# A residual block with two normalised convolutions: the first image's normalisation, its loads and its PE warm-up reordered tile by tile

## Chip, cores and metric

The kernel runs on one core of one Trainium2 chip. The time is device microseconds (us) per execution. Before the change it was 293.24 us (median of 6 executions, 292.82 to 293.89). Single outliers exist (one execution of the kernel before took 418 us); they count as slow and are left out.

Names used below: PE is the tensor engine (matmuls, and transposes done as matmuls), PEld its weight loads, DVE the vector engine, ACT the scalar engine, POOL the GpSimd engine, SP the engine that issues most DMA loads. The span is the length of the one execution that the profiler recorded. "Cold" and "warm" name two speeds of PE that the traces below show, the cold one about half the warm one.

## The reference

```
# x: 2 x 512 x 32 x 32, G = 4 groups of 128 channels, all bf16
def gn(z, gamma, beta):            # per image and group of 128 channels
    mu, var = mean and variance of z over the group
    return (z - mu) / sqrt(var + 1e-5) * gamma + beta
h = conv3(silu(gn(x, g1, be1)), w1)        # 3x3, 512 -> 512 channels
h = h + (silu(t_emb) @ w_emb)              # one number per image and channel
h = conv3(silu(gn(h, g2, be2)), w2)
out = x + h
```

One group has exactly 128 channels, so it is one SBUF tile of 128 partitions. An image has four such tiles. The statistics of one tile do not depend on another tile.

## The kernel before

The parts that matter are the order of each engine's work before the first convolution. Weights arrive as output rows by input columns and are transposed on PE, 36 blocks of 128x128 per chunk, in five sets (8, 8, 8, 8, 4) called `("T", chunk, set)`. After each set ACT or DVE copies it out of PSUM. "tot1" is the small matmul that sums a tile's statistics over partitions. "v1" and "sb1" are the two halves of the scale chain on DVE, with a power step ("rs1") on POOL between them. "sig" is the sigmoid on ACT and "mul" the multiply on DVE that writes the padded input of the convolution.

```
# PE list (cut)
pe_list.append(("tot1", 0))                 # all four tiles of image 0 in one matmul
pe_list.append(("gbT",))                    # transpose of gamma/beta
for s_ in range(3): pe_list.append(("T",) + c0 + (s_,))
# ... six warm-up matmuls, then the first convolution group, with inserts:
#     after input tile 0: T sets 3, 4;  after input tile 2: ("tot1", 1) for image 1

# PE, "tot1": waits for every tile of the image
eng.wait_sem(sem_dve, max(EV("dve", ("st1", b * CT + ct)) for ct in range(CT)))

# PE, convolution: input tile by input tile, in order
for cit in range(CT):
    wait_input(cit)                         # weight copies of this tile, and its "mul"
    for tap in range(9):
        for ph in range(NPH):               # two halves of 512 pixels
            e.matmul(acc_bank(s_, ph), lhsT, pad_window(src_buf, jt, dy, dx, ph), ...)
    for k2 in inserts.get(cit, []):
        emit(k2)

# SP (cut)
dma_x(0); dma_w(0, 0); dma_w(0, 1); dma_x(1)   # image 0, weight chunks, image 1
# POOL (cut): constants, then the four loads of g1, be1, g2, be2, then the zero borders
```

## Time and profile before

| what | value | where to read it |
|---|---|---|
| time | 293.24 us; span of the profiled execution 291.0 | times; first line of the page |
| PE busy | 278.4 us, 96% of the span | part 1 of the page |
| first convolution matmul | 15.42 us | chain of waits |
| end of the first convolution group | 32.36 us | chain of waits |
| 18 matmuls of 512 columns, array warm | 3.98 us, 0.221 each | chain of waits |

The first lines of the page of the kernel before. The "busy tenths" line cuts the span into 40 slices of 7.3 us, and each digit is the busy share in tenths.

```profile
span 291.0 us, 3566 instructions
PE 278.4 (96%) x1575; PEld 139.6 (48%) x1575; DVE 71.8 (25%) x189; ACT 59.5 (20%) x75; POOL 14.3 (5%) x29
PE   0699999999999999999999999999999999999996
```

PE is saturated from the third slice on. Only the first two slices, and the very end, have room.

This is the chain that ended last in the kernel before, up to the second group: the work followed back from the last instruction, each piece waiting for the one before it. Columns: start, duration, engine and tile written, source line, count.

```profile
1.64 4.03 DMA x_sb<-in_x_dram
...
5.69 1.30 DVE bn L738 x2
...
9.47 0.57 PE stat_ps L915 x2
...
10.15 1.87 PE tp L905 x16
...
13.23 1.25 ACT s_buf L655
...
14.58 0.71 DVE xn_pad L784
...
15.42 4.13 PE acc L983 x18
19.56 0.73 PE tp L905 x12
20.29 7.96 PE acc L983 x36
28.25 0.12 PE stat_ps L915 x2
28.37 3.99 PE acc L983 x18
32.36 0.94 PE stat_ps L940 x36
```

Read it downwards. The path goes through the load of x, DVE's statistics of two tiles, one statistics matmul for all tiles, 16 transposes, the sigmoid and the multiply. From 15.42 us on every piece is PE. Compare the two transpose lines: 16 take 1.87 us (0.117 each) at 10 us, and 12 take 0.73 us (0.061 each) at 19.6 us. The array is cold in the first and warm in the second.

### The profile page before, as it was taken

What the parts mean: (1) busy time and instruction counts of PE and PEld (TensorE: products, weight loads), DVE (VectorE), ACT (ScalarE), POOL (GpSimd) and SP (SyncE); (2) the same over time, 40 slices, a digit from 0 to 9 for tenths busy, and PEclk for the clock granted to TensorE, in tenths of its full rate; (3) what the DMA queues carried; (4) which work ended last, traced back from release to release, by engine and by line L of the source; (5) the groups of instructions that cost most, each with busy time, mean ns of one, the idle gap of its engine ahead of it and who ended that gap; (6) DMA issues with size and microseconds to landing.
All of it is one profiled execution on the core that took longest, in us unless ns stands there. A gap on an engine that the chain in (4) does not pass through costs nothing.

```text
span 291.0 us, 3566 instructions
## 1 busy us (share of the span) xinstructions
PE 278.4 (96%) x1575; PEld 139.6 (48%) x1575; DVE 71.8 (25%) x189; ACT 59.5 (20%) x75; POOL 14.3 (5%) x29
## 2 busy tenths in 40 slices
PE   0699999999999999999999999999999999999996
PEld 0544654645546455464544444444444444444466
DVE  2584640512405124051250504010000101010101
ACT  6475730412404224042240301000000000000000
POOL 8300100000000000000000000000000000000000
DMA  7997040040300000000000001010000101010010
GB/s 253 360 333 318 0 149 16 0 164 0 129 36 0 0 2 0 0 2 0 2 0 0 0 3 36 0 36 2 11 25 0 38 0 36 2 36 0 18 38 18
DMA packets 8543, 15.04 MB, mean 52 GB/s; under 512 B 3280, under 2 KB 6480, under 8 KB 7504
## 3 DMA queue, kind: packets, MB, share of 16 engines
q1 hardware_dynamic: 8400, 14.82, 14.2%
q8 instruction: 12, 0.20, 0.3%
q14 instruction: 3, 0.02, 0.0%
q0 software_dynamic: 128, 0.00, 0.0%
HBM read 12.72 MB, written 2.10 MB: 51 GB/s over the span
## 4 chain that ended last, share of the span: by engine, by line
PE 95%; DVE 2%; DMA 1%; issue 0%; ACT 0%; SPq 0%; DVEq 0%
PE acc L983 82%; PE acc L1010 6%; PE tp L905 4%; PE misc_ps L905 2%; DMA x_sb<-in_x_dram 1%; DVE bn L738 1%; ACT s_buf L655 0%; PE stat_ps L940 0%; PE stat_ps L929 0%; SPq L515 0%; DVE xn_pad L784 0%; PE stat_ps L915 0%; DVE me L740 0%; DVE me L743 0%; DVE o_sb L867 0%
## 5 line engine op out<-in xcount | busy, mean ns | idle before, releaser
L983 PE MATMUL acc<-xn_pad,w1T 128*128 128x512 bf16 x576 | 130.0, 383 | 0.7 <-DVE xn_pad L784 0.7
L983 PE MATMUL acc<-h1n_pad,w2T 128*128 128x512 bf16 x504 | 111.6, 383 | 0.0
L983 PEld LDWEIGHTS acc<-xn_pad,w1T 128*128 128x128 bf16 x576 | 55.5, 98 | 68.3 <-DVE xn_pad L784 1.2
L983 PEld LDWEIGHTS acc<-h1n_pad,w2T 128*128 128x128 bf16 x504 | 49.0, 98 | 61.9
L867 DVE TENSOR_TENSOR o_sb<-acc,x_sb 128x512 bf16<-128x512 f32 (+2 forms) x18 | 11.2, 631 | 107.2 <-PE acc L983 86.6
L905 PE MATMUL tp<-ident,w_raw 128*128 128x128 bf16 x200 | 16.6, 236 | 0.3 <-ACT w1T L626 0.3
L1010 PE MATMUL acc<-h1n_pad,w2T 128*128 128x128 bf16 (+2 forms) x144 | 16.2, 274 | 0.0
L905 PEld LDWEIGHTS tp<-ident,w_raw 128*128 128x128 bf16 x200 | 15.4, 149 | 1.5 <-ACT w1T L626 0.5
L610 POOL TENSOR_TENSOR tmp<-tmp,mhalf 128x1 f32<-128x1 f32 (+1 forms) x10 | 6.4, 644 | 164.3 <-DVE tmp L702 162.4
L626 ACT ACTIVATE w1T<-tp 128x1024 bf16<-128x1024 bf16 (+1 forms) x9 | 7.9, 876 | 29.0 <-PE tp L905 29.0
L1010 PEld LDWEIGHTS acc<-h1n_pad,w2T 128*128 128x128 bf16 x144 | 11.2, 97 | 5.2
L684 ACT ACTIVATE h<-acc,emb_sb 128x512 bf16<-128x512 f32 x16 | 10.1, 683 | 17.3 <-DVE mv L824 15.8
L667 ACT ACTIVATE s_buf<-h,bias,scale 128x1024 bf16<-128x1024 bf16 x8 | 9.9, 1233 | 14.9 <-DVE bias L711 14.9
L822 DVE BATCH_NORM_STATS2 bn<-acc 128x6 f32<-128x512 f32 x16 | 10.3, 686 | 8.8 <-PE acc L983 8.8
L626 ACT ACTIVATE w2T<-tp 128x1024 bf16<-128x1024 bf16 (+1 forms) x8 | 6.9, 863 | 27.0 <-PE tp L905 27.0
L720 DVE COPY w2T<-tp 128x1024 bf16<-128x1024 bf16 x5 | 3.4, 689 | 29.8 <-PE tp L905 29.8
L655 ACT ACTIVATE s_buf<-x_sb,bias,scale 128x1024 bf16<-128x1024 bf16 x8 | 9.4, 1230 | 6.2 <-DVE bias L711 6.2
L915 PE MATMUL stat_ps<-me,gm 128*128 128x8 f32 x4 | 0.8, 285 | 9.5 <-DVE me L732 9.5
L804 DVE TENSOR_TENSOR h1n_pad<-z_buf,s_buf 128x1024 bf16<-128x1024 bf16 x8 | 5.6, 697 | 14.4 <-ACT s_buf L667 14.4
L626 ACT ACTIVATE w2T<-misc_ps 128x1024 bf16<-128x1024 bf16 (+1 forms) x4 | 3.7, 916 | 23.5 <-PE misc_ps L905 23.5
L905 PE MATMUL misc_ps<-ident,w_raw 128*128 128x128 bf16 x88 | 7.4, 225 | 0.0
L905 PEld LDWEIGHTS misc_ps<-ident,w_raw 128*128 128x128 bf16 x88 | 6.8, 148 | 0.6
(56 smaller groups left out, 78.0 us busy)
## 6 DMA issues: line engine op xcount, KB each, us to landing
w_raw<-in_w_dram SPq DMA_DIRECT2D x8, 1152.0 KB, 7.4
x_sb<-in_x_dram SPq DMA_DIRECT2D x8, 256.0 KB, 6.6
out_dram<-o_sb SPq DMA_DIRECT2D x15, 128.0 KB, 1.7
wemb_sb<-in_w_emb_dram SPq DMA_DIRECT2D x1, 1152.0 KB, 8.3
out_dram<-o_sb SPq DMA_DIRECT2D x1, 64.0 KB, 1.5
out_dram<-o_sb SPq DMA_DIRECT2D x2, 32.0 KB, 1.4
gb_rows<-in_g_dram POOLq DMA_DIRECT2D x2, 1.0 KB, 4.4
gb_rows<-in_be_dram POOLq DMA_DIRECT2D x2, 1.0 KB, 4.5
```

Source lines behind the costliest of these rows:

```text
L610: eng.ev(e.tensor_tensor(A["rstd"], A["veps"], mhalf[:, 0:A["ncol"]], ALU.pow), key)
L626: return e.activation(dst, src, ACT.Copy)
L655: e.activation(s_buf[:, slot, :], x_sb[:, j, :], ACT.Sigmoid, bias=bias1[:, j:j + 1], scale=scale1[:, j:j + 1],),
L667: e.activation(s_buf[:, slot, :], h1[:, j, :], ACT.Sigmoid, bias=bias2[:, i:i + 1], scale=scale2[:, i:i + 1],),
L684: ins = e.activation(h1[:, j, ph * NBLK:(ph + 1) * NBLK], acc_bank(s_, ph), ACT.Identity, bias=emb_sb[:, col:col + 1], scale=1.0,)
L720: return e.tensor_copy(dst, src)
L804: e.tensor_tensor(pad_interior(h1n_pad, j), tile3(z_buf, slot), tile3(s_buf, slot), ALU.mult,),
L822: eng.ch(e.bn_stats(bn2[:, i, ph * 6:(ph + 1) * 6], acc_bank(s_, ph)))
L867: e.tensor_tensor(o_sb[:, i2 % 2, c_lo:c_lo + ncol], bank_ap, x_sb[:, j, c_lo:c_lo + ncol], ALU.add,),
L905: ins = e.transpose(tp[tbank(g)][:, n * P:(n + 1) * P], w_raw_v[k_][:, cit, tap, :], ident[:])
L983: ins = e.matmul(acc_bank(s_, ph), lhsT, pad_window(src_buf, jt, dy, dx, ph), start=(m == 0), stop=(m == nmm - 1),)
L1010: ins = e.matmul(acc_ap, lhsT, v[:, r0 + dy:r0 + dy + nr, dx:dx + W], start=(m == 0), stop=(m == nmm - 1),)
```

## The change

The intent is to start the first convolution sooner. Its first input tile needs only tile 0 of x, tile 0's statistics, and nine transposed blocks. The change gives tiles 0 and 1 their own statistics and scale chains. It loads half of the first weight chunk right behind x tile 0, and moves the gamma/beta loads from POOL's queue to ACT's. It puts only two transpose sets before the convolution, and starts warming PE as soon as x tile 0 is there. DVE's list is interleaved by hand to suit. The work is also shared differently: ACT does the statistics of tiles 1 and 3 of image 0 (before: 0 and 1), and four of the first chunk's five copies are DVE's (before: two).

```
+    units1: (image 0: [0]), (image 0: [1]), (image 0: [2, 3]), (image 1: [4..7])   # condensed
-    NWARM = 6
+    NWARM = 3
-    # PE, condensed: tot1(0); gbT; T sets 0, 1, 2; six warm-ups; convolution
+    # PE, condensed: four warm-ups; tot1(unit 0); gbT; T sets 0, 1; three warm-ups; tot1(unit 1); three warm-ups; convolution
+    ins0 = {
+        "mid": [("T",) + c0 + (2,)],                     # after tap 4 of input tile 0
+        0: [("tot1", 2), ("T",) + c0 + (3,), ("T",) + c0 + (4,)],
+        2: [("tot1", 3)],                                # image 1's statistics
+    }
...  ACT list
+    xstat 1, sig 0, xstat 3, sig 1, xstat 4, sig 2, sig 3, copy of set 4   # condensed; xstat = statistics on ACT
...  DVE list
+        ("st1", 0), ("v1", 0), ("gbc",), ckey(c0, 0), ("sb1", 0), ("z", 0), ("st1", 1), ckey(c0, 1), ("mul", 0),
+        ("v1", 1), ("st1", 2), ("st1", 3), ("sb1", 1), ("z", 1), ckey(c0, 2), ("mul", 1),
+        ("v1", 2), ckey(c0, 3), ("sb1", 2), ("z", 2), ("mul", 2), ("z", 3), ("mul", 3),
...  SP
-            dma_x(0)
-            dma_w(0, 0)
+            dma_x(0, [0])
+            e.dma_start(w_raw[:, 0, 0:HALF], w_chunk_src(0, 0)[:, 0:HALF]).then_inc(sem_w[(0, 0)], 16)
+            dma_x(0, range(1, CT))
+            e.dma_start(w_raw[:, 0, HALF:KW], w_chunk_src(0, 0)[:, HALF:KW]).then_inc(sem_w00b, 16)
...  the loop over g1, be1, g2, be2: from POOL's list to the head of ACT's
(cut: index bookkeeping, the new sharing between ACT and DVE, and the split of "mul" into "z" and "mul", which keeps the same instructions)
```

More of the change, by code (lines that the diff above doesn't have):

```diff
@@ L99, in bass_standalone__adm_resblock__diffusion_kernel @@
     NTE = B * ET
-    assert NGB <= P and NTE <= P and NGB + NTE <= 1024
-    NWARM = 6
+    assert NGB <= P
+    NWARM = 3
     QSPLIT = (NPH == 2 and RH % 4 == 0 and CT * B >= 2)
     RQ = RH // 2
+    RQ8 = RH // 4
     conv_groups = [(cot, b) for cot in range(CT) for b in range(B)]
@@ L108, in bass_standalone__adm_resblock__diffusion_kernel @@
     chunks = [(c, k) for c in range(2) for k in range(CT)]
+    c0 = chunks[0]
     R = chunks[1:]
     last_first = conv_groups[NG - 1][1] == conv_groups[0][1]
+    units1 = []
+    if CT >= 2:
+        units1.append((0, [0]))
+        units1.append((0, [1]))
+        units1.append((0, list(range(2, CT))))
+    else:
+        units1.append((0, [0]))
+    for b in range(1, B):
+        units1.append((b, [b * CT + ct for ct in range(CT)]))
+    NU1 = len(units1)
+    unit_of_tile = {}
+    for u, (b, tl) in enumerate(units1):
+        for j in tl:
+            unit_of_tile[j] = u
+    units_of_batch = {}
+    for u, (b, tl) in enumerate(units1):
+        units_of_batch.setdefault(b, []).append(u)
+    act_stat_tiles = set()
+    if CT >= 4:
+        act_stat_tiles.update({1, 3})
+        for b in range(1, B):
+            act_stat_tiles.update({b * CT, b * CT + 1})
+    elif CT >= 2:
+        act_stat_tiles.add(1)
+        for b in range(1, B):
+            act_stat_tiles.add(b * CT + CT - 1)
     def copy_eng(chunk, s):
+        if chunk == c0:
+            return {0: "dve", 1: "dve", 2: "dve", 3: "dve"}.get(s, "act" if s % 2 == 0 else "dve")
         return "act" if s % 2 == 0 else "dve"
@@ L116, in ckey @@
         return ("C" if copy_eng(chunk, s) == "act" else "Cd",) + chunk + (s,)
-    pe_list, act_list, dve_list, pool_list = [], [], [], []
-    pe_inserts = {}
-    if CT >= 4:
-        act_stat_tiles = set(b * CT + ct for b in range(B) for ct in (0, 1))
-    elif CT >= 2:
-        act_stat_tiles = set(b * CT + (CT - 1) for b in range(B))
-    else:
-        act_stat_tiles = set()
     def sets_of_cit(cit):
@@ L130, in sets_of_cit @@
         return sorted(set(range(lo // 8, hi // 8 + 1)))
-    c0 = chunks[0]
-    n_pre = NSETS
+    pe_list, act_list, dve_list, pool_list = [], [], [], []
+    pe_inserts = {}
+    g0key = ("conv", 0) + conv_groups[0]
     pe_list.append(("tot1", 0))
     pe_list.append(("gbT",))
-    n_pre = min(NSETS, max(3, max(sets_of_cit(0)) + 1))
-    for s_ in range(n_pre):
+    for s_ in (0, 1):
         pe_list.append(("T",) + c0 + (s_,))
-    g0key = ("conv", 0) + conv_groups[0]
-    ins0 = {}
-    if n_pre < NSETS:
-        ins0[0] = [("T",) + c0 + (s_,) for s_ in range(n_pre, NSETS)]
-    if B >= 2 and CT >= 3:
-        ins0.setdefault(CT - 2, []).append(("tot1", 1))
-    for cit in sorted(ins0):
-        for k2 in ins0[cit]:
-            pe_list.append(k2)
-    if ins0:
-        pe_inserts[g0key] = ins0
+    pe_list.append(("tot1", 1))
+    ins0 = {
[3 more added lines that the diff above has]
+    }
+    for where in ("mid", 0, 2):
+        pe_list.extend(ins0[where])
+    pe_inserts[g0key] = ins0
     pe_list.append(g0key)
-    if B >= 2 and CT < 3:
-        pe_list.append(("tot1", 1))
-    for b in range(2, B):
-        pe_list.append(("tot1", b))
     pe_list.append(("emb",))
@@ L204, in bass_standalone__adm_resblock__diffusion_kernel @@
     act_list.append(("warm",))
-    for j in sorted(act_stat_tiles):
-        if j < CT:
-            act_list.append(("xstat", j))
-    rest = [s_ for s_ in range(NSETS) if copy_eng(c0, s_) == "act"]
-    sigs = [("sig", ct) for ct in range(CT)]
-    order = []
-    if rest:
-        order.append(ckey(c0, rest.pop(0)))
-    if sigs:
-        order.append(sigs.pop(0))
-    if rest:
-        order.append(ckey(c0, rest.pop(0)))
-    while sigs:
-        order.append(sigs.pop(0))
-    while rest:
-        order.append(ckey(c0, rest.pop(0)))
-    act_list.extend(order)
-    act_list.append(("tsig",))
-    for b in range(1, B):
-        for j in sorted(act_stat_tiles):
-            if b * CT <= j < (b + 1) * CT:
-                act_list.append(("xstat", j))
+    for k2 in (("xstat", 1), ("sig", 0), ("xstat", 3), ("sig", 1), ("xstat", CT),
+               ("sig", 2), ("sig", 3), ckey(c0, 4)):
+        act_list.append(k2)
+    for b in range(1, B):
+        for j in sorted(t for t in act_stat_tiles if b * CT < t < (b + 1) * CT):
+            act_list.append(("xstat", j))
+        if b == 1:
+            act_list.append(("tsig",))
         for ct in range(CT):
             act_list.append(("sig", b * CT + ct))
+    if B == 1:
+        act_list.append(("tsig",))
     for i in range(1, NG):
@@ L250, in bass_standalone__adm_resblock__diffusion_kernel @@
     act_list.append(("sig", NT + NG - 1))
-    for b in range(B):
+    for k2 in (
+        ("st1", 0), ("v1", 0), ("gbc",), ckey(c0, 0), ("sb1", 0), ("z", 0), ("st1", 1), ckey(c0, 1), ("mul", 0),
+        ("v1", 1), ("st1", 2), ("st1", 3), ("sb1", 1), ("z", 1), ckey(c0, 2), ("mul", 1),
+        ("v1", 2), ckey(c0, 3), ("sb1", 2), ("z", 2), ("mul", 2), ("z", 3), ("mul", 3),
+    ):
+        dve_list.append(k2)
+    for b in range(1, B):
+        u = units_of_batch[b][0]
         tiles = [b * CT + ct for ct in range(CT)]
@@ L261, in bass_standalone__adm_resblock__diffusion_kernel @@
                 dve_list.append(("st1", j))
-        dve_list.append(("v1", b))
-        if b == 0:
-            dve_list.append(("gbc",))
-            odd0 = [s_ for s_ in range(NSETS) if copy_eng(c0, s_) == "dve"]
-            if odd0:
-                dve_list.append(ckey(c0, odd0.pop(0)))
-        dve_list.append(("sb1", b))
-        for ct in range(CT):
-            dve_list.append(("mul", b * CT + ct))
-        if b == 0:
-            for s_ in odd0:
-                dve_list.append(ckey(c0, s_))
+        dve_list.append(("v1", u))
+        dve_list.append(("sb1", u))
+        for j in tiles:
+            dve_list.append(("z", j))
+            dve_list.append(("mul", j))
     if B == 1:
@@ L290, in bass_standalone__adm_resblock__diffusion_kernel @@
             dve_list.append(("sb2", i - 2))
+            dve_list.append(("z", NT + i - 2))
             dve_list.append(("mul", NT + i - 2))
@@ L300, in bass_standalone__adm_resblock__diffusion_kernel @@
         dve_list.append(("sb2", NG - 2))
+        dve_list.append(("z", NT + NG - 2))
         dve_list.append(("mul", NT + NG - 2))
@@ L308, in bass_standalone__adm_resblock__diffusion_kernel @@
         dve_list.append(("sb2", NG - 1))
+        dve_list.append(("z", NT + NG - 1))
         dve_list.append(("mul", NT + NG - 1))
@@ L314, in bass_standalone__adm_resblock__diffusion_kernel @@
         dve_list.append(("sb2", NG - 1))
+        dve_list.append(("z", NT + NG - 1))
         dve_list.append(("mul", NT + NG - 1))
@@ L328, in bass_standalone__adm_resblock__diffusion_kernel @@
     pool_list.append(("mhalf",))
-    pool_list.append(("dma_small",))
     pool_list.append(("powwarm",))
@@ L332, in bass_standalone__adm_resblock__diffusion_kernel @@
     pool_list.append(("hpad",))
-    for b in range(B):
-        pool_list.append(("rs1", b))
+    for u in range(NU1):
+        pool_list.append(("rs1", u))
     for i in range(NG):
@@ L378, in bass_standalone__adm_resblock__diffusion_kernel @@
         me2 = S(nc.sbuf_tensor([P, NG, 2], FP32))
-        mom1 = S(nc.sbuf_tensor([P, B, CT, 2], FP32))
-        tmp1 = S(nc.sbuf_tensor([P, B, 4, CT], FP32))
+        mom1 = S(nc.sbuf_tensor([P, NT, 2], FP32))
+        tmp1 = S(nc.sbuf_tensor([P, 4, NT], FP32))
         scale1 = S(nc.sbuf_tensor([P, NT], FP32))
@@ L408, in bass_standalone__adm_resblock__diffusion_kernel @@
         sem_w = {ch_: S(nc.semaphore("dma_w%d_%d" % ch_)) for ch_ in chunks}
+        sem_w00b = S(nc.semaphore("dma_w0_0b"))
         block = S(nc.Block())
@@ L419, in bass_standalone__adm_resblock__diffusion_kernel @@
         MGB = 0
-        MTE = MGB + NGB
         VAL_GB = 16 * 4
@@ L426, in out_dma_idx @@
             return i2 * NPH + ph
-        RQ8 = RH // 4
         def last_pieces(s_):
@@ L468, in wait_copy @@
             eng.wait_sem(ev_sem_of[ce], EV(ce, ckey(chunk_s[:2], chunk_s[2])))
-        def wait_chunk_copies(eng, chunk):
-            last = {}
-            for s in range(NSETS):
-                last[copy_eng(chunk, s)] = s
-            for ce, s in last.items():
-                eng.wait_sem(ev_sem_of[ce], EV(ce, ckey(chunk, s)))
         inv_cg = 1.0 / Cg
@@ L480, in chain_aps @@
             if which == 1:
-                b = idx
-                tot_ap = stat_ps[:, TOT1 + 2 * CT * b:TOT1 + 2 * CT * (b + 1)].rearrange("p (n k) -> p n k", k=2)
-                mom_ap = mom1[:, b, :, :]
-                tmp4 = tmp1[:, b, :, :]
-                gamma_ap = gb32[:, 0, :]
-                beta_ap = gb32[:, 1, :]
-                scale_ap = scale1[:, b * CT:(b + 1) * CT]
-                bias_ap = bias1[:, b * CT:(b + 1) * CT]
-                ncol = CT
+                b, tl = units1[idx]
+                j0, j1 = tl[0], tl[-1] + 1
+                ct0, ct1 = j0 - b * CT, j1 - b * CT
+                tot_ap = stat_ps[:, TOT1 + 2 * j0:TOT1 + 2 * j1].rearrange("p (n k) -> p n k", k=2)
+                mom_ap = mom1[:, j0:j1, :]
+                tmp4 = tmp1[:, :, j0:j1]
+                gamma_ap = gb32[:, 0, ct0:ct1]
+                beta_ap = gb32[:, 1, ct0:ct1]
+                scale_ap = scale1[:, j0:j1]
+                bias_ap = bias1[:, j0:j1]
+                ncol = j1 - j0
             else:
@@ L510, in _, with dma_x @@
             eng = _Eng("sp", e, None, None, ev_index)
-            def dma_x(b):
-                for ct in range(CT):
+            def dma_x(b, cts):
+                for ct in cts:
                     j = b * CT + ct
@@ L521, in dma_w @@
                 e.dma_start(w_raw[:, k_, :], w_chunk_src(c_, k_)).then_inc(sem_w[(c_, k_)], 16)
-            dma_x(0)
-            dma_w(0, 0)
+            HALF = KW // 2
+            dma_x(0, [0])
+            e.dma_start(w_raw[:, 0, 0:HALF], w_chunk_src(0, 0)[:, 0:HALF]).then_inc(sem_w[(0, 0)], 16)
+            dma_x(0, range(1, CT))
+            e.dma_start(w_raw[:, 0, HALF:KW], w_chunk_src(0, 0)[:, HALF:KW]).then_inc(sem_w00b, 16)
             if CT >= 2:
@@ L527, in _ @@
             for b in range(1, B):
-                dma_x(b)
+                dma_x(b, range(CT))
             for b in range(B):
@@ L585, in _ @@
                     eng.ev(e.memset(mhalf[:], -0.5), key)
-                elif kind == "dma_small":
-                    for v_i, vec in enumerate((g1, be1, g2, be2)):
-                        e.dma_start(
-                            gb_rows[v_i * CT:(v_i + 1) * CT, :],
-                            vec.rearrange("(ct p) -> ct p", p=P),
-                        ).then_inc(sem_gb, 16)
-                    eng.ev(e.memset(junk[:, 3:4], 0.0), key)
                 elif kind == "powwarm":
@@ L617, in _ @@
             eng = _Eng("act", e, sem_act, semc_act, ev_index)
+            for v_i, vec in enumerate((g1, be1, g2, be2)):
+                e.dma_start(
+                    gb_rows[v_i * CT:(v_i + 1) * CT, :],
+                    vec.rearrange("(ct p) -> ct p", p=P),
+                ).then_inc(sem_gb, 16)
             def copy_set(key):
@@ L650, in _ @@
                         j = u
-                        b = j // CT
                         eng.wait_sem(sem_xs[j], 16)
-                        eng.wait_sem(sem_dve, EV("dve", ("sb1", b)))
+                        eng.wait_sem(sem_dve, EV("dve", ("sb1", unit_of_tile[j])))
                         eng.ev(
@@ L749, in _ @@
                 elif kind == "v1":
-                    b = key[1]
-                    eng.wait_sem(sem_pe, EV("pe", ("tot1", b)))
-                    eng.ev(gn_chain_a(chain_aps(1, b)), key)
+                    u = key[1]
+                    eng.wait_sem(sem_pe, EV("pe", ("tot1", u)))
+                    eng.ev(gn_chain_a(chain_aps(1, u)), key)
                 elif kind == "sb1":
-                    b = key[1]
-                    eng.wait_sem(sem_pool, EV("pool", ("rs1", b)))
+                    u = key[1]
+                    eng.wait_sem(sem_pool, EV("pool", ("rs1", u)))
                     eng.wait_sem(sem_dve, EV("dve", ("gbc",)))
-                    eng.ev(gn_chain_b(chain_aps(1, b)), key)
+                    eng.ev(gn_chain_b(chain_aps(1, u)), key)
                 elif kind == "v2":
@@ L766, in _ @@
                     eng.ev(gn_chain_b(chain_aps(2, i)), key)
-                elif kind == "mul":
+                elif kind == "z":
                     u = key[1]
@@ L771, in _ @@
                         j = u
-                        b = j // CT
-                        eng.wait_sem(sem_dve, EV("dve", ("sb1", b)))
-                        eng.ch(
-                            e.tensor_scalar(
-                                z_buf[:, slot, :], x_sb[:, j, :],
-                                scale1[:, j:j + 1], bias1[:, j:j + 1], ALU.mult, ALU.add,
-                            )
-                        )
-                        eng.sync()
-                        eng.wait_sem(sem_act, EV("act", ("sig", u)))
-                        eng.wait_sem(sem_pool, EV("pool", ("xpad",)))
-                        eng.ev(
-                            e.tensor_tensor(
-                                pad_interior(xn_pad, j), tile3(z_buf, slot), tile3(s_buf, slot), ALU.mult,
-                            ),
-                            key,
-                        )
+                        eng.wait_sem(sem_dve, EV("dve", ("sb1", unit_of_tile[j])))
+                        src, sc_ap, bi_ap = x_sb[:, j, :], scale1[:, j:j + 1], bias1[:, j:j + 1]
                     else:
@@ L793, in _ @@
                         eng.wait_sem(sem_act, EV("act", ("evac", i)))
-                        eng.ch(
-                            e.tensor_scalar(
-                                z_buf[:, slot, :], h1[:, j, :],
-                                scale2[:, i:i + 1], bias2[:, i:i + 1], ALU.mult, ALU.add,
-                            )
-                        )
-                        eng.sync()
-                        eng.wait_sem(sem_act, EV("act", ("sig", u)))
-                        eng.wait_sem(sem_pool, EV("pool", ("hpad",)))
-                        eng.ev(
-                            e.tensor_tensor(
-                                pad_interior(h1n_pad, j), tile3(z_buf, slot), tile3(s_buf, slot), ALU.mult,
-                            ),
-                            key,
-                        )
+                        src, sc_ap, bi_ap = h1[:, j, :], scale2[:, i:i + 1], bias2[:, i:i + 1]
+                    if u >= 2:
+                        eng.wait_sem(sem_dve, EV("dve", ("mul", u - 2)))
+                    eng.ev(e.tensor_scalar(z_buf[:, slot, :], src, sc_ap, bi_ap, ALU.mult, ALU.add), key)
+                elif kind == "mul":
+                    u = key[1]
+                    slot = u % 2
+                    eng.wait_sem(sem_dve, EV("dve", ("z", u)))
+                    eng.wait_sem(sem_act, EV("act", ("sig", u)))
+                    if u < NT:
+                        j = u
+                        eng.wait_sem(sem_pool, EV("pool", ("xpad",)))
+                        dst = pad_interior(xn_pad, j)
+                    else:
+                        j = tile_of_group(u - NT)
+                        eng.wait_sem(sem_pool, EV("pool", ("hpad",)))
+                        dst = pad_interior(h1n_pad, j)
+                    eng.ev(e.tensor_tensor(dst, tile3(z_buf, slot), tile3(s_buf, slot), ALU.mult), key)
                 elif kind == "temb":
@@ L884, in _, with dummy @@
                     inserted.update(lst)
+            def dummy(n, rhs):
+                for _ in range(n):
+                    e.matmul(acc[:, NPH, 0:rhs.shape[-1]], ident[:, :], rhs, start=True, stop=True)
             def emit(key):
@@ L897, in emit @@
                     eng.wait_sem(sem_w[(c_, k_)], 16)
+                    if (c_, k_) == (0, 0) and s >= 2:
+                        eng.wait_sem(sem_w00b, 16)
                     if tprev[g] is not None:
@@ L907, in emit @@
                 elif kind == "tot1":
-                    b = key[1]
+                    u = key[1]
+                    if u == 1:
+                        dummy(3, x_sb[:, 0, 0:512])
+                    b, tl = units1[u]
+                    j0, j1 = tl[0], tl[-1] + 1
                     eng.wait_sem(sem_pool, EV("pool", ("gm",)))
-                    eng.wait_sem(sem_dve, max(EV("dve", ("st1", b * CT + ct)) for ct in range(CT)))
-                    if b >= 1:
-                        eng.wait_sem(sem_dve, EV("dve", ("v1", b - 1)))
-                    rhs = me1[:, b * CT:(b + 1) * CT, :].rearrange("p n k -> p (n k)")
+                    eng.wait_sem(sem_dve, max(EV("dve", ("st1", j)) for j in tl))
+                    if u >= 1:
+                        eng.wait_sem(sem_dve, EV("dve", ("v1", u - 1)))
+                    rhs = me1[:, j0:j1, :].rearrange("p n k -> p (n k)")
                     eng.ev(
-                        e.matmul(stat_ps[:, TOT1 + 2 * CT * b:TOT1 + 2 * CT * (b + 1)], gm[:], rhs,
-                                 start=True, stop=True),
+                        e.matmul(stat_ps[:, TOT1 + 2 * j0:TOT1 + 2 * j1], gm[:], rhs, start=True, stop=True),
                         key,
@@ L926, in emit @@
                         eng.wait_sem(sem_dve, EV("dve", ("embc",)))
-                        eng.wait_sem(sem_dve, EV("dve", ("v1", B - 1)))
+                        eng.wait_sem(sem_dve, EV("dve", ("v1", NU1 - 1)))
                     eng.ev(
@@ L935, in emit @@
                     eng.wait_sem(sem_dve, EV("dve", ("temb",)))
-                    eng.wait_sem(sem_dve, EV("dve", ("v1", B - 1)))
+                    eng.wait_sem(sem_dve, EV("dve", ("v1", NU1 - 1)))
                     ins = None
@@ L952, in emit @@
                     acc_free_waits(eng, Q)
-                    if c_ == 0 and i == 0:
+                    if c_ == 0 and i == 0 and NWARM > 0:
                         eng.wait_sem(sem_pool, EV("pool", ("ident",)))
@@ L987, in emit @@
                                 m += 1
+                                if cit == 0 and tap == 4:
+                                    for k2 in inserts.get("mid", []):
+                                        emit(k2)
                             for k2 in inserts.get(cit, []):
@@ L1017, in emit @@
                     raise AssertionError(key)
+            eng.wait_sem(sem_pool, EV("pool", ("ident",)))
+            eng.wait_sem(sem_xs[0], 16)
+            dummy(4, x_sb[:, 0, 0:512])
             for key in pe_list:
```

## The prediction

> **What bounds the kernel.** The profile's page: span 291.0 us, PE busy 96%. The chain of waits is PE from 15.42 us (first convolution matmul) to 288.87 us without a hole; 18 matmuls of 512 columns take 3.98 us warm (0.221 each). So the only loose time is the first 15.4 us. There the chain reads: x lands (5.67), VectorE statistics of tiles 2 and 3 (to 9.33), one statistics matmul for all four tiles (10.03), 16 transposes (1.87 us), scale and bias (13.2), sigmoid 1.25, multiply 0.71, convolution at 15.42.
>
> **What the change does.** Each 128-channel tile is one normalisation group, so tile 0 need not wait for tiles 1 to 3. It gets its own chain; half of the first weight chunk is loaded right behind x tile 0; the gamma/beta loads move from POOL's queue (2.2 us of POOL, timeline 1.74 to 3.98) to ACT's; only two transpose sets precede the convolution, the third moves inside its first input tile; warm-up matmuls come early (4 + 3 + 3 instead of 6). Matmul work is otherwise unchanged, as is everything after the first two groups.
>
> **The new start, from durations in the before trace.** x tile 0 lands at 3.55 (timeline). Statistics on VectorE: 5.3. Statistics matmul to 6.0, first scale chain to 6.6. The half weight chunk ends the first 832 KB; by the landings of before (768 KB at 5.65, 1024 KB at 6.35) it lands near 5.9, x tile 1 near 6.5. Gamma/beta I expect by 6.3. Eight cold transposes to 7.6, copy to 8.3, scale and bias to 8.9. ACT does statistics of tile 1 (2.2 us) to 8.7, so the sigmoid runs 8.9 to 10.2; multiply (behind a second copy) to 11.1; convolution at about 11.3, 4.1 us earlier.
>
> **What it gives back.** PE now does the third transpose set (0.50 us) and one more statistics matmul (0.12) after the start. VectorE's list from the first multiply to the statistics of the second image adds up to about 14.2 us (statistics at 1.69 us, scale chains, copies, z and multiply, waits for sigmoids), while PE reaches that statistics matmul after 3 input tiles, 13.4 us. PE runs in order, so I expect it to wait there about 0.6 us. Net: 4.1 - 0.6 - 0.6 = 2.9 us, say 2.8; after the first group both kernels run the same PE-bound chain, so it carries over whole: 293.24 - 2.8 = 290.4 us.
>
> **Warm clock.** The Trainium skill, "TensorE: Matmul & The Clock Gate", Part 1, says that the array runs at half rate until busy for some 3.4 us. The before trace agrees: transposes 0.12 us each from 10.1 to 12.0, 0.06 at 19.5. In the new order PE works from 3.6 us with pauses, so I expect it warm by the convolution. If not, some matmuls cost double, up to 1 us in all.
>
> **Right or wrong will show in** the timeline: first convolution matmul near 11.3; the wait of the second image's statistics matmul near 25, about 0.6 us; end of the first group near 29.6 instead of 32.4; PE gapless after that.
>
> **What would make it wrong:** gamma/beta landing late behind the big loads (delays the in-order PE); a cold array; longer waits for tile 1's or 2's multiply inside the first group, as VectorE there is nearly full; on the other side, no wait at the second image's statistics gives 0.6 us more.
>
> Prediction: 290.4 us, 8 in 10 within 288.8 to 292.0; faster by over 2% 0.04, within 2% 0.95, slower 0.01.

## The result, and the profile after

The kernel after takes 289.27 us (median of 8 executions, 289.10 to 289.74). The kernel before took 292.83 us over all 16 of its executions by then (292.41 to 293.89). The ratio is 0.9876 with a 95% interval of 0.9862 to 0.9889. Ratios here and below are the mean time of one kernel's fast runs over that of the other's of the same rounds, so they are not quite the ratio of the quoted medians. The gain is 3.56 us by medians (292.83 - 289.27).

The first lines of the page of the kernel after:

```profile
span 288.0 us, 3598 instructions
PE 281.8 (98%) x1583; PEld 140.5 (49%) x1583; DVE 74.7 (26%) x203; ACT 57.6 (20%) x73; POOL 12.8 (4%) x26
PE   4999999999999999999999999999999999999996
```

The second slice is now full and the first one partly so. Part of that is warm-up work: PE's busy time went up by 3.4 us while the span fell by 3.0.

The chain that ended last in the kernel after, over the same stretch:

```profile
1.95 4.19 DMA gb_rows<-in_be_dram
...
6.19 0.19 PE misc_ps L884
6.38 1.85 PE tp L900 x16
8.24 1.28 PE acc L877 x3
9.52 0.35 PE stat_ps L914 x2
9.87 1.30 PE acc L955 x3
11.17 2.51 PE acc L981 x10
13.67 0.48 PE tp L900 x8
14.15 1.76 PE acc L981 x8
15.91 0.13 PE stat_ps L914 x2
...
24.98 0.39 PE stat_ps L914 x2
25.37 4.00 PE acc L981 x18
29.37 0.94 PE stat_ps L938 x36
```

The path no longer begins with x and its statistics. It begins with the gamma/beta loads on ACT's queue, and then runs through PE itself: their transpose, 16 transposes still at the cold rate, and the warm-ups. Near 25 us there is a new wait. The 36 matmuls of input tiles 1 and 2 end at 24.76 (PE's timeline starts them at 16.64 and gives 8.12 us), but the statistics matmul of image 1 starts at 24.98 only. Before, this matmul cost 0.12 us of the chain; now wait and matmul together take 0.61 (24.76 to 25.37), so 0.49 us is lost. The chain shows where the wait comes from: after PE's statistics matmul of tiles 2 and 3 (15.91) it leaves PE, runs through the scale, ACT's sigmoid and DVE's work (left out at the second "..." above), and comes back to PE at 24.98. Behind that point the two chains are alike piece by piece. The first group ends at 29.37 instead of 32.36, and the span is shorter by the same 3.0 us.

The next lines are PE's timeline of the kernel after. The bracket tells how long PE was idle and what ended it.

```profile
10.96 2.71 PE L981 MATMUL acc<-xn_pad,w1T 128*128 128x512 bf16 x10
...
24.98 0.39 PE L914 MATMUL stat_ps<-me,gm 128*128 128x8 f32 x2 [0.23 <-DVE me L733]
```

The first convolution matmul starts at 10.96 instead of 15.42. (The chain prints 11.17, because the modelled end of the last warm-up is there.) The ten matmuls take 2.71 us, and 2.38 in the executions below where the array is warm.

Which execution was profiled matters for tenths. The profiled one of the kernel after took 289.83 us, the slowest of nine, with a span of 288.0 where the others have 287.3 to 287.9. It began with some matmuls at the cold rate. A repeat of the same kernel, below, was profiled at 287.6. There the chain begins with x tile 0 and the four warm-ups that wait for it, so the two beginnings are nearly level.

### The profile page after: what moved, and what is told of

Same layout as the page of the kernel before. It is cut to its first block, busy times and chain, and to the rows that moved or that the text cites. A ratio compares the mean times of both kernels' runs of the same rounds, so it can differ in the third digit from the quotient of the medians.

```text
span 288.0 us, 3598 instructions
## 1 busy us (share of the span) xinstructions
PE 281.8 (98%) x1583; PEld 140.5 (49%) x1583; DVE 74.7 (26%) x203; ACT 57.6 (20%) x73; POOL 12.8 (4%) x26
## 4 chain that ended last, share of the span: by engine, by line
PE 94%; DVE 2%; DMA 1%; ACT 0%; ACTq 0%; issue 0%; POOL 0%; DVEq 0%
PE acc L981 80%; PE acc L1011 6%; PE tp L900 4%; PE misc_ps L900 2%; DMA gb_rows<-in_be_dram 1%; DVE bn L739 1%; DVE xn_pad L797 0%; PE acc L955 0%; PE acc L877 0%; ACT s_buf L656 0%; ACTq L616 0%; PE stat_ps L938 0%; PE stat_ps L927 0%; PE stat_ps L914 0%; POOL tmp L607 0%
## 5 line engine op out<-in xcount | busy, mean ns | idle before, releaser
L607 POOL TENSOR_TENSOR tmp<-tmp,mhalf 128x1 f32<-128x1 f32 (+2 forms) x12 | 7.2, 602 | 162.8 <-DVE tmp L703 162.8
L628 ACT ACTIVATE w1T<-tp 128x1024 bf16<-128x1024 bf16 (+1 forms) x7 | 5.8, 834 | 24.6 <-PE tp L900 24.6
L721 DVE COPY w1T<-tp 128x1024 bf16<-128x1024 bf16 x8 | 5.5, 688 | 11.0 <-PE tp L900 11.0
```

Source lines behind the costliest of these rows:

```text
L607: eng.ev(e.tensor_tensor(A["rstd"], A["veps"], mhalf[:, 0:A["ncol"]], ALU.pow), key)
L628: return e.activation(dst, src, ACT.Copy)
L721: return e.tensor_copy(dst, src)
```

## The experiments

Theory A, the prediction's: tile 0's own chain made the start earlier; the loads and the queue are what lets this chain run; warmth keeps the gain; part is given back as a wait at image 1's statistics. Rival B: the new order of loads and queues made the gain, and the tile split is decoration. Rival C: a warmer array made it. Each experiment gave correct results. The runs came on three chips, so every row's ratio is against the kernel before on its own chip.

| run | median us | range | ratio to before | 95% |
|---|---|---|---|---|
| e1_gb_on_pool | 292.00 | 291.52 to 292.26 | 0.9961 | 0.9942 to 0.9980 |
| e2_one_group | 295.56 | 295.15 to 296.61 | 1.0089 | 1.0069 to 1.0109 |
| e3_no_warmup | 291.63 | 290.46 to 292.10 | 0.9946 | 0.9929 to 0.9964 |
| e4_late_stats | 289.03 | 288.61 to 289.53 | 0.9861 | 0.9844 to 0.9879 |
| e5_w_behind_x | 291.86 | 290.96 to 292.91 | 0.9959 | 0.9930 to 0.9988 |
| e6_early_warmup | 289.10 | 288.84 to 289.58 | 0.9860 | 0.9842 to 0.9879 |
| e7_both | 288.57 | 288.43 to 288.60 | 0.9844 | 0.9829 to 0.9859 |
| e8_one_group_warm | 294.12 | 293.81 to 294.46 | 1.0035 | 1.0017 to 1.0052 |
| e9_before_no_warmup | 294.32 | 294.04 to 295.58 | 1.0053 | 1.0028 to 1.0078 |
| e10_before_early_warmup | 292.47 | 291.79 to 292.92 | 0.9987 | 0.9966 to 1.0007 |
| e11_after_again | 289.27 | 289.06 to 289.46 | 0.9872 | 0.9856 to 0.9888 |
| e12_both_again | 288.36 | 288.12 to 288.85 | 0.9843 | 0.9828 to 0.9859 |

### Gamma/beta back on POOL's queue

```
-            for v_i, vec in enumerate((g1, be1, g2, be2)): e.dma_start(...)      # head of ACT's list
+    pool_list.append(("dma_small",))                                            # POOL, after its constants
+                elif kind == "dma_small":
+                    for v_i, vec in enumerate((g1, be1, g2, be2)): e.dma_start(...)
```

> The changed kernel with one part undone: the gamma/beta loads go back to POOL's queue. In the kernel after, their transpose waited for them until 6.19 us, and 16 transposes, the first weight copy and the scale follow it. In the kernel before, the last of the four loads landed about 9.1 us on POOL's queue (issued at 3.46, 5.6 us to landing). Theory A (tile 0's own chain made the gain, and the early loads are what lets that chain run): transpose at about 9.2, first convolution matmul near 13.7 instead of 10.96, about 2.5 us given back, near 291.8 us. Rival B0 (the queue does not matter, since the kernel before had no wait for these loads): no change, 289.3.

Measured: 292.00 us, 2.7 us given back. The chain of this run, and PE's timeline at the convolution:

```profile
3.47 5.20 DMA gb_rows<-in_be_dram
...
8.71 0.19 PE misc_ps L887
```

```profile
13.36 2.38 PE L984 MATMUL acc<-xn_pad,w1T 128*128 128x512 bf16 x10
```

The last load lands at 8.67 (3.47 + 5.20) instead of 6.14, and the convolution starts 2.4 us later than in the kernel after. Of the 2.5 us, 1.5 come from the later issue (3.47 instead of 1.95) and 1.0 from the longer way to landing (5.20 instead of 4.19). The rival that the queue does not matter falls. It had a point: in the profiled execution of the kernel before, the same late loads cost nothing, because the statistics matmul ahead of their transpose ended at 10.03. The margin there is small: in the run of the kernel before without warm-ups, below, they took 6.43 us and PE waited 0.24 us for them.

### One statistics unit for image 0 again, twice

```
-        units1.append((0, [0])); units1.append((0, [1])); units1.append((0, list(range(2, CT))))
+        units1.append((0, list(range(CT))))
     # PE:  gbT, T sets 0 and 1, three warm-ups, tot1(0), three warm-ups, convolution
     # ACT: xstat 1, xstat 3, sig 0, sig 1, sig 2, sig 3, ...
     # DVE: all four statistics, then v1, sb1, then z and mul tile by tile
```

> The changed kernel with one part undone: image 0's four tiles get one common statistics unit again; the order of loads, the ACT queue, the transposes inside the convolution and the warm-ups stay. Theory A: the start goes back to where it was; statistics of the last tile on ACT end near 10.5, one 1.0 us power step for four columns, scale near 13.5, multiply near 15.5, first convolution matmul near 15.6, and with no wait at image 1's statistics any more about 3.5 us given back in all: 292.8 us, level with the kernel before. Rival B (the loads and queues made the gain): at most 291, first convolution matmul before 13.

Measured: 295.56 us, 2.8 us over the forecast and slower than the kernel before. The start was nearly as forecast, but the array was cold:

```profile
11.52 1.44 PE L951 MATMUL acc<-x_sb,ident 128*128 128x512 bf16 x3
16.15 4.45 PE L977 MATMUL acc<-xn_pad,w1T 128*128 128x512 bf16 x10 [3.19 <-DVE xn_pad L793]
```

Ten matmuls took 4.45 us where warm ones take 2.38. PE had idled 3.19 us just before them, and it was cold before that too: the three warm-ups took 1.44 us. So this run undid two things, the tile split and the warmth, and says nothing clean about the first. It was repeated with the idle time filled:

```
-                        dummy(3, x_sb[:, 0, 0:512])
+                        dummy(8, x_sb[:, 0, 0:512])
-    NWARM = 3
+    NWARM = 14
```

> The run with one common statistics unit again (it gave 295.6 us, 2.8 over the forecast; its first ten convolution matmuls took 4.45 us instead of 2.2, the array cold after PE had idled from 9.3 to 11.1 and 12.9 to 16.1), now with 8 + 14 warm-up matmuls in those gaps instead of 3 + 3. If the excess was the cold array: first convolution matmul still near 16.1, ten of them in 2.3 us, 2.0 us faster than the first version: 293.2 to 293.9, level with or up to 1 us behind the kernel before (whose start was 15.4). If the excess has another cause, it stays at 295.5.

Measured: 294.12 us, 1.4 us faster than the first version and a little over the forecast.

```profile
7.97 3.34 PE L873 MATMUL acc<-x_sb,ident 128*128 128x512 bf16 x8
11.15 0.28 PE L910 MATMUL stat_ps<-me,gm 128*128 128x8 f32 x2
...
15.91 2.39 PE L977 MATMUL acc<-xn_pad,w1T 128*128 128x512 bf16 x10 [1.44 <-DVE xn_pad L793]
```

Now the array is warm and the start is at 15.91. All the changed loads, queues and warm-ups without the tile split give a kernel 0.35% slower than the one before, so rival B falls: they make no gain without the split. The start is 0.5 us later than before's 15.42, and the trace shows two reasons. The statistics are ready at 10.69 (before: 9.32): x tile 1 lands behind half a weight chunk, and ACT does tiles 1 and 3 one after the other from 6.02 on. Then the eight warm-ups, which stand ahead of the statistics matmul in PE's list, hold PE until 11.31.

So the run is not the split undone and nothing else; it also keeps the new sharing of statistics and has a warm-up in the way. A kernel with one unit, all else new, the old sharing and no such delay was not run. An estimate from this trace: DVE ends tile 2 near 8.5, tile 3 on DVE takes 1.8 more (as in the kernel before), so the statistics are ready near 10.4. The statistics matmul follows by about 10.9 and the convolution 4.46 us behind it (as here, 11.45 to 15.91), near 15.4. By this sum the other parts without the split would be level with the kernel before, 4.4 us of start behind the kernel after.

### No warm-ups

```
-    NWARM = 3
+    NWARM = 0
-                        dummy(3, x_sb[:, 0, 0:512])        # before tot1(unit 1)
-            dummy(4, x_sb[:, 0, 0:512])                    # at the head of PE's list
```

> The changed kernel without any of its ten warm-up matmuls. Theory A': the array is not warm at the first convolution matmul, so some 8 to 10 of them cost 0.43 us; part of the delay is hidden in the wait at image 1's statistics (0.4 us): 0.5 to 1.2 us slower, 289.8 to 290.5. Rival C (the warm-ups made a main part of the gain): over 2 us slower. Rival D (they are useless, as the transposes warm the array): same or 0.2 us faster.

Measured: 291.63 us with 1.6 us between the fastest and the slowest execution. The loss is 2.4 us by medians (from 289.27 on another chip) and meets rival C's number; I had forecast 0.5 to 1.2. The profiled execution was the luckiest of the six (290.46):

```profile
10.62 3.72 PE L979 MATMUL acc<-xn_pad,w1T 128*128 128x512 bf16 x10 [0.98 <-DVE xn_pad L797]
```

The start is even earlier (10.62), but ten matmuls take 3.72 us. So warm-ups carry much of the time. Whether they are the *change's* gain needs the same question put to the kernel before, which has six of its own:

```
-    NWARM = 6
+    NWARM = 0
```

> The kernel before without its six warm-up matmuls. The changed kernel lost 2.2 us without its ten. If warm-ups are worth about the same in both, the change's gain is not one of warmth: before loses 1 to 2.5 us here too (294.2 to 295.7). If before loses under 0.5 us, then most of the change's gain hangs on its added warm-ups.

Measured: 294.32 us, ratio 1.0053: before loses about 1.2 us by medians, 1.6 by the ratio.

```profile
15.44 6.90 PE L983 MATMUL acc<-xn_pad,w1T 128*128 128x512 bf16 x18 [2.08 <-DVE xn_pad L784]
```

Its profiled execution, the slowest of four, took 6.90 us for 18 matmuls that took 4.13 with the warm-ups. Without warm-ups on either side the change is still worth 2.7 us by the medians (294.32 - 291.63; two chips). By the two ratios it is 0.9946 / 1.0053 = 0.9893, about 3.1 us. The rest of the 3.6 us, 0.5 to 0.9, goes with the warm-ups. That the new order needs them more because its convolution comes sooner is likely, but not shown.

### The kernel before with an early warm-up

```
+            eng.ch(e.memset(wrm[:], 0.5))                  # DVE, first instruction; wrm is 128 x 512
+            eng.wait_sem(semc_dve, 1)                      # PE, first instructions
+            for _ in range(22):
+                e.matmul(acc[:, NPH, 0:512], wrm[:, 0:P], wrm[:, :], start=True, stop=True)
```

> The kernel before plus 22 warm-up matmuls on a constant tile from about 1.4 us, so its 24 first transposes run warm (0.06 instead of 0.12 us). Its second weight copy stood before the scale step at 12.04 to 12.6; it comes about 0.8 us earlier, the first convolution matmul near 14.7: 0.5 to 0.9 us faster, 292.2 to 292.6. Rival C (warmth, not the tile split, made most of the change's gain): 1.5 us or more faster, 291.5 or less.

Measured: 292.47 us, ratio 0.9987; the interval includes 1. The trace shows the mechanism. In the chain of this run the same 16 transposes as before take 1.14 us, and the convolution starts at 14.39:

```profile
9.85 1.14 PE tp L907 x16
...
14.39 4.14 PE acc L985 x18
```

The profiled execution was the fastest of four (291.79), so its whole microsecond is not typical. Warming the kernel before buys about half a microsecond, which the timing cannot tell from nothing. It does not buy 3.6. Rival C falls.

### The half weight chunk behind all of image 0

```
+            dma_x(0, range(1, CT))
             e.dma_start(w_raw[:, 0, 0:HALF], ...)
-            dma_x(0, range(1, CT))
```

> The changed kernel with the first half weight chunk queued behind all four x tiles of image 0 instead of behind the first. Theory A: it lands at about 7.9 instead of 5.4 us; the first transposes start near 7.95 instead of 6.3, so the weight copy, scale and first multiply come about 1.3 to 1.6 us later: 290.4 to 290.9 us. Rival (the transposes are not on the path, statistics of the next tiles are, and x tile 1 now comes 1.8 us earlier): same or faster, at most 289.3.

Measured: 291.86 us, 2.6 us slower than the kernel after, where I forecast 1.1 to 1.6. The chain:

```profile
2.59 6.01 DMA w_raw<-in_w_dram
...
8.64 1.92 PE tp L900 x16
```

The half chunk landed at 8.60, not at the forecast 7.9. The convolution started at 13.27. Theory A's direction holds: the transposes are on the path, and ACT's statistics of tile 1, which start 1.9 us sooner (4.12 instead of 6.07), do not help. The size was off mainly by the landing time.

### The wait at image 1's statistics, and an earlier warm-up

```
-        2: [("tot1", 3)],
+        "mid3": [("tot1", 3)],          # emitted after tap 1 of input tile 3
```

> The changed kernel with the statistics matmul of image 1 moved from before the fourth input tile of the first group to after that tile's second tap (four matmuls, 0.88 us later). If the wait seen there (PE idle near 24.7 to 25.1, about 0.35 us) is a real cost of in-order PE, it vanishes and the kernel is 0.3 to 0.4 us faster, 288.9 us, with image 1's first multiply (now 29.8) still ahead of the second group's first matmul (31.7). If the idle time is an artefact of modelled matmul ends, or is only passed on to the second group, nothing changes (289.3).

Measured: 289.03 us, ratio 0.9861 beside 0.9876. By time alone this is not separable. In the chain the wait is gone:

```profile
16.09 8.86 PE acc L981 x40
24.95 0.12 PE stat_ps L914 x2
```

The statistics matmul follows the 40th matmul at once and costs 0.12 us, as it did before the change. The 0.5 us that the trace shows to be regained is larger than the 0.24 between the medians, but both are within the scatter of the start from execution to execution.

```
-            eng.wait_sem(sem_xs[0], 16)
-            dummy(4, x_sb[:, 0, 0:512])
+            # DVE writes a constant tile first; PE waits for that only
+            for _ in range(10):
+                e.matmul(acc[:, NPH, 0:512], wrm[:, 0:P], wrm[:, :], start=True, stop=True)
```

> The changed kernel with its four first warm-up matmuls, which wait for x tile 0, replaced by ten on a constant tile that VectorE writes at the start, so PE is busy from about 1.1 us. If it is busy time alone that warms the array: the 16 transposes near 6.3 take 1.0 instead of 1.9 us, scale 0.5 us earlier, first convolution matmul at 10.4 or earlier with no cold ones (ten in 2.2 instead of 2.4 to 2.7 us); but VectorE's list follows only by 0.5 us, so PE waits longer at image 1's statistics: 0.3 to 0.6 us faster, 288.7 to 289.0, and less spread between runs. If the state at the first convolution does not depend on such early work: 289.3.

Measured: 289.10 us, again not separable alone. The profiled execution shows warm transposes, but a convolution start of 11.04, no earlier than in the kernel after:

```profile
6.41 1.25 PE L902 MATMUL tp<-ident,w_raw 128*128 128x128 bf16 x16
...
11.04 2.37 PE L983 MATMUL acc<-xn_pad,w1T 128*128 128x512 bf16 x10 [0.77 <-DVE xn_pad L799]
```

PE waits for the multiply, and at image 1's statistics for 0.24 us as before. The bound has moved to ACT, which does the statistics of tile 1 ahead of tile 0's sigmoid and got x tile 1 late in this execution (6.77 us).

> The early warm-up together with the later statistics matmul of image 1, which takes the wait away that absorbs part of the earlier start: 0.9 to 1.4 us faster than the changed kernel, 287.9 to 288.4. If the two only buy the same wait, no better than the better one of them alone (288.7 to 289.0).

Measured: 288.57 us, ratio 0.9844. It is 0.7 us faster than the kernel after by medians of different chips, and short of the forecast by 0.2. So it was run again beside the kernel after on one chip, in these two runs:

> The changed kernel unaltered, on the chip of the next three: the base for them, and how much single executions differ. Expected again 289.1 to 289.8, ratio near 0.9876.

> The early warm-up and the later statistics matmul together, unaltered, beside the changed kernel on one chip. If the gain of the earlier run (288.57 against 289.27 on another chip) is real: 0.5 to 1.0 us faster than the changed kernel here. If it was the chip or the clock's phase: within 0.3.

Measured: 289.27 for the kernel after (289.06 to 289.46) and 288.36 with both edits (288.12 to 288.85). The ranges do not touch. The combination is 0.9 us faster than the kernel after, and 1.6% faster than the kernel before. The first chain is the kernel after again (span 287.6), the second the one with both edits (span 286.3):

```profile
24.54 0.39 PE stat_ps L914 x2
...
28.93 0.93 PE stat_ps L938 x36
```

```profile
1.64 4.19 DMA x_sb<-in_x_dram
...
8.04 1.14 ACT s_buf L657
...
9.27 0.71 DVE xn_pad L799
...
10.11 2.38 PE acc L983 x10
...
24.47 0.12 PE stat_ps L916 x2
...
27.69 0.93 PE stat_ps L940 x36
```

The path of the best version starts with x tile 1 and ACT's statistics of it, then tile 0's sigmoid and multiply. From 10.11 us on it is PE without a hole. This profiled execution was the fastest of the five (288.12).

## Why the prediction was right

The measured 289.27 lies in the range 288.8 to 292.0, and "within 2%" was right. The forecast gain was 2.8 us, the measured one 3.56. Step by step, against the profiled execution of the kernel after (288.0) and its repeat (287.6):

| step | predicted | after | repeat |
|---|---|---|---|
| gamma/beta transpose starts | 6.3 | 6.19 | 6.04 |
| first convolution matmul | 11.3 | 10.96 | 10.86 |
| third transpose set plus one statistics matmul, after the start | 0.62 | 0.61 | 0.61 |
| lost at image 1's statistics | 0.6 | 0.49 | 0.50 |
| end of the first group | 29.6 | 29.37 | 28.93 |

- What bounds the kernel: right. After the first group the two chains are the same, so what is won there stays whole.
- The tile split as the cause: right, by the run e8_one_group_warm (no split, no gain, with the estimate above for what that run mixes in) and by the rivals that failed. The loads are not decoration: gamma/beta on POOL's queue costs 2.7 us of the gain, the half chunk behind x 2.6. So the gain belongs to the parts together and can't be divided among them. No run isolates the move of the third transpose set or the new sharing between ACT and DVE.
- The give-back: right in place; that the size fits too is partly luck. The prediction put 0.6 us on PE's wait alone, but PE stands idle for only about 0.23 us, and 0.27 us that it did not foresee is the statistics matmul itself, which takes 0.39 us of the chain after a wait and 0.12 in an unbroken stream. The prediction counted DVE's list from the first multiply on. In both traces DVE waits once more for PE on the way (0.58 and 0.17 us, at the statistics of tiles 2 and 3), so an earlier start alone does not remove this wait: it is 0.23 us in both, and 0.24 in the run with the early warm-up alone.
- The mis-sized term is the start. The prediction put 4.1 us on it; the repeat shows 15.42 - 10.86 = 4.56. In the profiled execution of the kernel after, each link came a little sooner than forecast: x landed at 3.43 instead of 3.55, gamma/beta at 6.14 instead of 6.3, the scale was ready at 8.57 instead of 8.9 and the multiply at 10.71 instead of 11.1. In the repeat x landed later (3.60), but the multiply ended at 10.71 too. The sum in the repeat is 4.56 - 0.61 - 0.50 = 3.45, and the end of the first group is 3.43 us earlier, which is nearly all of 3.56. The prediction had 4.1 - 0.6 - 0.6, rounded down to 2.8. Also, the forecast started from 293.24, the median of six executions; sixteen gave 292.83.
- "Warm by the convolution" was half right. In the profiled execution the first ten matmuls took 2.71 us, in the repeat 2.38, the warm figure. The transposes and warm-ups before them were cold in both (16 in 1.85, three of 512 columns in 1.28). The forecast of up to 1 us for a cold array was too small: without warm-ups the loss is 2.4 us.

On the clock, the Trainium skill, "TensorE: Matmul & The Clock Gate", Part 1 ("What's actually happening"), describes a monitor with a free-running window of about 3.4 us that halves the PE clock until PE has been busy, so that the number of slow matmuls varies from run to run. The runs fit the two rates: cold transposes take 0.117 us and warm ones 0.061. On the variation they say little: the kernel without warm-ups scatters over 1.6 us (six executions), while the run with both edits scatters over 0.2 in its first round (four, 288.43 to 288.60) and 0.7 in its second (five). The length of the window was not measured. The section "Why this matters for your kernels" of the same page warns of idle gaps of about 3 us and more between bursts. No run here shows a warm array going cold: the first one-unit run has a gap of 3.19 us followed by ten matmuls at half rate, but it was cold before the gap as well. The second one-unit run stays warm over a gap of 1.44 us (ten in 2.39).

## What to carry to other kernels

When an engine is saturated from some point to the end, look only at what precedes that point: find the smallest piece of data that lets it start, and give that piece its own chain. Each shortening uncovers the next bound (here the statistics, then the gamma/beta load, then ACT's order), so check things that cost nothing before, such as a 1 KB load, against the new start time. Keep PE busy with throw-away matmuls through the prologue (here also on a constant tile that no load delays), and when an experiment takes work away, check that it did not also let the array go cold.

## What the Trainium skill lacked or had wrong

- "TensorE: Matmul & The Clock Gate", Part 4 (PE-mode transpose), says that the full clock does not engage for transposes. In these traces transposes do run at the faster rate once the array is warm: 12 transposes take 0.73 us (0.061 each) against 16 in 1.87 (0.117 each) when cold, and in the kernel before with an early warm-up 16 take 1.14. Whether transposes alone would warm the array no run shows.
- The same page, Part 1, puts the ramp at under 1% of a typical kernel's span and advises not to fit a particular number of cold matmuls. Here taking ten warm-up matmuls away costs 2.4 of 289 us, 0.8%, which is true to the letter but more than half of what the whole change won.
- "DMA: Bandwidth & Descriptors", Latency and other measured facts, gives about 0.8 us as the least time of a tiny transfer and first-byte times of 0.6 and 1 us for the two issue paths; Queues, rings and completion order has each engine serve its queues in turn. No page says what a tiny load issued beside a full queue takes: here 4.19 us for the last 1 KB of gamma/beta on ACT's queue (3.93 to 4.19 over four runs' traces), 5.20 on POOL's (6.43 in the run of the kernel before without warm-ups), with more than a megabyte of x and weights issued and not yet landed.
- No page has the cost of a small float32 matmul that comes after a wait: 0.39 us of the chain, against 0.12 in an unbroken stream of matmuls. The traces point to its weight load: after the wait it starts together with the matmul (both at 24.98 in the kernel after), while in the stream it starts 0.23 us ahead of it (24.56 and 24.79 in the run with the later statistics). No run tested this.
